# Transposing C for one of two weight tables with TensorE instead of the DMA queue, in a four-layer SSM kernel

## The chip, the cores and the metric

The kernel runs on one core of a Trainium2 chip. The metric is the device time of one execution in microseconds. Each core has TensorE (PE, matrix multiply), VectorE (DVE), ScalarE (ACT), GpSimd (POOL) and SyncE (SP, which here only issues DMA), with two on-chip memories: SBUF, and PSUM, into which PE writes its results.

## The reference, cut to what matters

Four layers alternate over a sequence of 2048 tokens with 640 features, in bfloat16: A, B, A, B. Each begins with a layer norm and adds its result to its input.

```python
def _A_ref(x, Lambda_re, Lambda_im, B_re, B_im, C_re, C_im, log_dt, Dskip):
    Lam_bar = jnp.exp(dt * Lam)                               # one complex number for each state
    B_bar = ((Lam_bar - 1.0) / Lam)[:, None] * Bmat
    Bu = jnp.einsum("bld,pd->blp", x + 0j, B_bar)
    for t in range(L):
        h = Lam_bar[None, :] * h + Bu[:, t, :]
        hs.append(h)
    return 2.0 * jnp.einsum("blp,dp->bld", hseq, Cmat).real + x * Dskip

def _B_ref(q, k, v, shift_k, ssm_k, ssm_D):
    kv = (short convolution of k with shift_k) * v
    y = (long convolution of kv with ssm_k, by FFT) + kv * ssm_D
    return q * y

x = x + _A_ref(_layernorm(x), ...)      # A1
x = x + _B_ref(_layernorm(x), ...)      # B1
x = x + _A_ref(_layernorm(x), ...)      # A2
x = x + _B_ref(_layernorm(x), ...)      # B2
```

Both A layers have the same parameters, and both B layers the same k, v and filters, so the long convolution y is computed once.

## The kernel before

The kernel has three stages, which overlap. The set-up makes tables of the parameters of A. The y passes (five, of 128 features each) compute the long convolution with matrix products. Then the layers run, each in four chunks of 512 tokens.

In layer A the recurrence runs over pairs of tokens. It needs the transposed B in two forms (BT0, BT1), two tables of C, transposed and scaled (W0 and W1), a product of W0 with B (G0), and tables of cosines and sines (tab, rtab). All are made once and used by every chunk. W0 and W1 each have a real and an imaginary part, of five blocks of 128 rows; each block is a column block of C, transposed, in a linear combination of its real and imaginary parts with one scalar per row. In the kernel before, each block of C is transposed by the DMA on its way in, separately for W0 and W1:

```python
    R_wr = Ring(St["b5"], 2, lambda t: (t[:, 0:2 * D].rearrange("p (c d) -> p c d", c=2), t[:, 2 * D:4 * D].bitcast(F32)))
    def weights(w, after):
        made = []
        for j in range(NJ):
            s_wr = R_wr.new()
            t_wl = []
            for c, src in ((0, A_C_re), (1, A_C_im)):
                def e_wl(_, c=c, src=src, j=j, s_wr=s_wr):
                    nc.sync.dma_start_transpose(out=s_wr.get()[0][:, c, :], in_=src[:, j * P:(j + 1) * P])        # L549
                t_wl.append(S.add(f"a_wl{w}{j}:{c}", "sp", 1.2, t_go, e_wl, xt=0.8, uses=[s_wr]))
            for c in range(2):
                def e_wc(...):
                    nc.scalar.activation(s_wr.get()[1], s_wr.get()[0][:, 1, :], ACT.Copy, scale=st["F6"][:, w, c + 1, j:j + 1])   # L553
                ...
                def e_wm(...):
                    nc.vector.scalar_tensor_tensor(aw["W1" if w else "W0"][:, c, j, :], s_wr.get()[0][:, 0, :],
                                                   st["F6"][:, w, c, j:j + 1], s_wr.get()[1], ALU.mult, ALU.add)          # L557
                ...
    w0s = weights(0, [])
    ...                                   # B transposed (a_b0, a_b1), then G0 from W0 and B (a_gm, a_ge)
    w1s = weights(1, gms)
```

B is loaded in whole rows and transposed by TensorE: a matmul with B as the stationary operand and the identity as the moving one (L573). Before the layers need them, W1[:, 0] and tab serve as homes of B, which is needed until the a_gm products are made; W1 is written after those.

PSUM is four buffers of 128 x 1024 f32. A matmul group takes one, and the copy out of it to SBUF, by ACT (L383) or DVE (L385), gives it back:

```python
def evac(nc, eng, out, in_):
    if eng == "act":
        nc.scalar.activation(out, in_, ACT.Copy)        # L383
    else:
        nc.vector.tensor_copy(out, in_)                 # L385
```

Other lines that are named below: L1172 is the short convolution of k and L1178 its product with v; L1217, L1241 to L1246, L1322/1323 and L1351 are matmuls of the y passes; L771 and L774 are the input products of layer A, L809 its scan and L860 its output products; L868 and L872 take the output products out of PSUM, L872 with the residual.

Each engine works through its own instructions in order. This order is made when the program is built. Every operation has a name and a number in a table; a list scheduler with estimated durations takes the operation that is ready and has the lowest number. Where an operation may run on two engines, a second number says how long to wait for the first:

```python
WHEN = {
    "warm": -3.83, "yt_io0": 2.11, ..., "a_wl00:0": 32.6, "a_wl00:1": 49.01, ..., "B2c3_st:3": 348.96,
}
```

The end of the program is the last chunk of layer B2. It is done in four sub-chunks, each of which waits for one output group (A2c3_cp) of layer A. Sub-chunks 0 to 2 normalise (L727 on ACT), multiply by y (L924 on DVE) and add x (L932 on DVE or GpSimd, for the last two chunks). Sub-chunk 3 has two fused DVE instructions (L909, L913), of which only the second needs the reciprocal (L692). Each sub-chunk is stored by its own DMA.

Of the kernel before, what the change touches and what calls it, by code (L numbers as in the profile page):

```python
# [9 lines left out]
ALU = mybir.AluOpType  # L10
# [7 lines left out]
P = 128  # L18
# [34 lines left out]
    "warm": -3.83, "yt_io0": 2.11, "yt_ph0": 2.86, "yt_sin0": 5.82, "yt_neg0": 16.74, "yt_io6": 1.83, "yt_ph6": 8.35, "yt_sin6": 13.55, "yt_neg6": 16.04,  # L53
    "yt_io12": 8.66, "yt_ph12": 10.58, "yt_sin12": 11.04, "yt_neg12": 16.39, "yt_Ci": 8.52, "yt_Si": 23.89, "yt_nsi": 31.06, "yt_f0": 1.21, "yt_f2": 6.25,
    "yt_f3": 9.49, "yt_f4": 8.15, "yt_h0": 0, "yt_h1": -0.99, "yt_h2": 5.01, "yt_h3": 5.6, "kv_dsl": 2.5, "kv_kd": 0.96, "kv_k0": 5.85, "kv_k1": 6.47,
    "kv_k2": 9.75, "kv_d0": 9.95, "kv_d1": 10.69, "kv_d2": 9.55, "kv_ds0": 12.7, "kv_lk0": -2.5, "kv_lv0": 12.92, "kv_mm0:0": 14.98, "kv_ev0:0": 17.09,
    "kv_mm0:1": 16.97, "kv_ev0:1": 19.32, "kv_st0": 19.31, "kv_ds1": 14, "kv_lk1": 18.02, "kv_lv1": 17.66, "kv_mm1:0": 20.91, "kv_ev1:0": 23.08,
    "kv_mm1:1": 22.64, "kv_ev1:1": 25.83, "kv_st1": 34.93, "kv_ds2": 15.3, "kv_lk2": 38.27, "kv_lv2": 32.7, "kv_mm2:0": 46.93, "kv_ev2:0": 49.89,
    "kv_mm2:1": 47.83, "kv_ev2:1": 50.31, "kv_st2": 52.4, "kv_ds3": 29.13, "kv_lk3": 49.12, "kv_lv3": 44.01, "kv_mm3:0": 57.23, "kv_ev3:0": 59.86,
    "kv_mm3:1": 55.5, "kv_ev3:1": 57.95, "kv_st3": 89.09, "kv_ds4": 59.54, "kv_lk4": 63.8, "kv_lv4": 68.5, "kv_mm4:0": 72.02, "kv_ev4:0": 76.44,  # L60
    "kv_mm4:1": 69.17, "kv_ev4:1": 73.75, "kv_st4": 85.43, "a_pl": 0, "a_p0": 11.98, "a_p1": 12.7, "a_p2": 14.74, "a_p3": 15.74, "a_p4": 18.22, "a_p5":
    20.49, "a_p6": 24.21, "a_lamd": 24.71, "a_f": 26.96, "a_dd": 13.22, "a_ldB0": 7.86, "a_ldB1": -0.25, "a_wl00:0": 32.6, "a_wl00:1": 49.01, "a_wc00:0":
    52.65, "a_wm00:0": 55.99, "a_wc00:1": 58, "a_wm00:1": 59.08, "a_wl01:0": 36.12, "a_wl01:1": 41.24, "a_wc01:0": 46.96, "a_wm01:0": 39.62, "a_wc01:1":
    45.93, "a_wm01:1": 52.05, "a_wl02:0": 55.3, "a_wl02:1": 54.1, "a_wc02:0": 59.45, "a_wm02:0": 60.99, "a_wc02:1": 62, "a_wm02:1": 63.6, "a_wl03:0":
    61.4, "a_wl03:1": 62.6, "a_wc03:0": 66.32, "a_wm03:0": 72.97, "a_wc03:1": 74.16, "a_wm03:1": 75.66, "a_wl04:0": 66.1, "a_wl04:1": 67.3, "a_wc04:0":
    73.44, "a_wm04:0": 74.88, "a_wc04:1": 76.91, "a_wm04:1": 78.89, "a_b00:0": 24.39, "a_b0e0:0": (25.02, -1), "a_b00:1": 18.7, "a_b0e0:1": (19.33, 99),
    "a_b00:2": 19.83, "a_b0e0:2": (19.91, 3), "a_b00:3": 24.96, "a_b0e0:3": (25.65, 99), "a_b00:4": 41.45, "a_b0e0:4": (42.57, 1.5), "a_b01:0": 7.78,
    "a_b0e1:0": (8.33, 99), "a_b01:1": 11.2, "a_b0e1:1": (17.24, 3), "a_b01:2": 8.91, "a_b0e1:2": (10.1, 1.5), "a_b01:3": 7.5, "a_b0e1:3": (8.91, 6),
    "a_b01:4": 9.82, "a_b0e1:4": (10.46, 99), "a_b10:0": 31.05, "a_b1e0:0": (32.11, 3), "a_b10:1": 34.44, "a_b1e0:1": (35.71, 1.5), "a_b10:2": 34.09,
    "a_b1e0:2": (34.05, 6), "a_b10:3": 29.71, "a_b1e0:3": 30.83, "a_b10:4": 26.83, "a_b1e0:4": (28.08, 99), "a_b11:0": 29.02, "a_b1e1:0": (29.24, 3),  # L70
    "a_b11:1": 38.81, "a_b1e1:1": (39.48, 6), "a_b11:2": 27.39, "a_b1e1:2": (28.66, 0), "a_b11:3": 32.04, "a_b1e1:3": (33.19, 3), "a_b11:4": 41.73,
    "a_b1e1:4": (43.23, 1.5), "a_gm0": 79.89, "a_ge0": (82.96, 0.8), "a_gm1": 89.66, "a_ge1": (93.72, 0.8), "a_gm2": 103.17, "a_ge2": (105.9, 99),
    "a_gm3": 93.91, "a_ge3": (98.25, 3), "a_gm4": 87.15, "a_ge4": (89.6, 3), "a_wl10:0": 78.7, "a_wl10:1": 102.7, "a_wc10:0": 110.77, "a_wm10:0": 114.1,
    "a_wc10:1": 125.39, "a_wm10:1": 133.68, "a_wl11:0": 87.7, "a_wl11:1": 84.7, "a_wc11:0": 89.2, "a_wm11:0": 106.96, "a_wc11:1": 113.29, "a_wm11:1":
    114.88, "a_wl12:0": 125.81, "a_wl12:1": 127, "a_wc12:0": 129.1, "a_wm12:0": 131.85, "a_wc12:1": 129.33, "a_wm12:1": 134.54, "a_wl13:0": 136.24,
    "a_wl13:1": 134.55, "a_wc13:0": 138.41, "a_wm13:0": 143.56, "a_wc13:1": 145.4, "a_wm13:1": 150.76, "a_wl14:0": 142.49, "a_wl14:1": 144.61, "a_wc14:0":
    148.81, "a_wm14:0": 150.98, "a_wc14:1": 153.51, "a_wm14:1": 155.99, "a_ti": 21.15, "a_ta": 22.89, "a_t0": 28.86, "a_t1": 116.09, "a_t2": 118.28,
    "yq0_kl": 4.7, "yq0_ka": 10.39, "yq0_KA:m0": 13.91, "yq0_KA:e0": (14.91, 0), "yq0_KA:m1": 16.88, "yq0_KA:e1": (17.73, 0.8), "yq0_KA:m2": 11.55,
    "yq0_KA:e2": (12.48, 0), "yq0_KA:m3": 11.83, "yq0_KA:e3": (13.61, 0.8), "yq0_KB:m0": 19.69, "yq0_KB:e0": (21.5, 0.8), "yq0_KB:m1": 25.93, "yq0_KB:e1":
    (27.18, 3), "yq0_KB:m2": 27.95, "yq0_KB:e2": (30.14, 99), "yq0_KB:m3": 19.26, "yq0_KB:e3": (20.51, -1), "yq0_KB:m4": 24.73, "yq0_KB:e4": (26.28, 99),  # L80
    "yq0_vl": 20.25, "yq0_VA:m0": 31.93, "yq0_VA:e0": (32.86, 0.8), "yq0_VA:m1": 31.61, "yq0_VA:e1": (31.78, -1), "yq0_VA:m2": 33.58, "yq0_VA:e2": (33.88,
    0.8), "yq0_VA:m3": 33.17, "yq0_VA:e3": (34.03, -1), "yq0_VB:m0": 36.93, "yq0_VB:e0": (37.23, 0), "yq0_VB:m1": 34.74, "yq0_VB:e1": 35.93, "yq0_VB:m2":
    34.86, "yq0_VB:e2": (38.43, 3), "yq0_VB:m3": 38.85, "yq0_VB:e3": (40.09, 3), "yq0_VB:m4": 40.15, "yq0_VB:e4": (40.99, 99), "yq1_kl": 28.9, "yq1_ka":
    35.09, "yq1_KA:m0": 39.77, "yq1_KA:e0": (40.4, -1), "yq1_KA:m1": 40.48, "yq1_KA:e1": (41.28, 0), "yq1_KA:m2": 34.56, "yq1_KA:e2": (36.44, 1.5),
    "yq1_KA:m3": 38.26, "yq1_KA:e3": 39.21, "yq1_KB:m0": 47.16, "yq1_KB:e0": (48.45, 0), "yq1_KB:m1": 43.41, "yq1_KB:e1": (45, 6), "yq1_KB:m2": 44.31,
    "yq1_KB:e2": (45.9, 6), "yq1_KB:m3": 42.51, "yq1_KB:e3": (40.68, 1.5), "yq1_KB:m4": 45.2, "yq1_KB:e4": (47.91, 0), "yq0_pw": 44.47, "yq0_IB:m0":
    41.73, "yq0_IB:e0": (50.06, 0), "yq0_IB:m1": 53.02, "yq0_IB:e1": (54.27, 0), "yq0_IB:m2": 50.53, "yq0_IB:e2": (53, 3), "yq0_IB:m3": 52.12,
    "yq0_IB:e3": (53.37, 6), "yq0_IB:m4": 51, "yq0_IB:e4": (52.12, 6), "yq0_tt": 56.5, "yq1_vl": 40.21, "yq1_VA:m0": 55.2, "yq1_VA:e0": (57.1, 3),
    "yq1_VA:m1": 52.74, "yq1_VA:e1": (53.85, -1), "yq1_VA:m2": 54.63, "yq1_VA:e2": (55.97, 0), "yq1_VA:m3": 54.92, "yq1_VA:e3": (56.77, 0), "yq1_VB:m0":
    61.7, "yq1_VB:e0": (62.72, 0.8), "yq1_VB:m1": 59.86, "yq1_VB:e1": (61.1, 99), "yq1_VB:m2": 60.8, "yq1_VB:e2": 62.14, "yq1_VB:m3": 58.96, "yq1_VB:e3":  # L90
    60.2, "yq1_VB:m4": 62.41, "yq1_VB:e4": (63.27, -1), "yq0_IA:m0": 65.86, "yq0_IA:e0": (70.73, 99), "yq0_IA:m1": 65.37, "yq0_IA:e1": 67.04, "yq0_st":
    73.4, "yq2_kl": 46.52, "yq2_ka": 53.61, "yq2_KA:m0": 63.88, "yq2_KA:e0": (64.52, 1.5), "yq2_KA:m1": 62.99, "yq2_KA:e1": (63.62, 99), "yq2_KA:m2":
    63.6, "yq2_KA:e2": (64.38, 0), "yq2_KA:m3": 64.76, "yq2_KA:e3": (65.42, 1.5), "yq2_KB:m0": 66.7, "yq2_KB:e0": (67.94, -1), "yq2_KB:m1": 71.13,
    "yq2_KB:e1": (72.54, 0), "yq2_KB:m2": 68.27, "yq2_KB:e2": (69.89, 6), "yq2_KB:m3": 67.37, "yq2_KB:e3": 68.99, "yq2_KB:m4": 69.96, "yq2_KB:e4": 72.04,
    "yq1_pw": 65.51, "yq1_IB:m0": 77.79, "yq1_IB:e0": (78.82, 99), "yq1_IB:m1": 76.23, "yq1_IB:e1": (77.63, 0.8), "yq1_IB:m2": 74.65, "yq1_IB:e2": (75.9,
    0), "yq1_IB:m3": 73.75, "yq1_IB:e3": (75, 3), "yq1_IB:m4": 75.82, "yq1_IB:e4": (78.53, 6), "yq1_tt": 79.9, "yq2_vl": 70.8, "yq2_VA:m0": 79.49,
    "yq2_VA:e0": (80.74, -1), "yq2_VA:m1": 78.92, "yq2_VA:e1": (80.07, 1.5), "yq2_VA:m2": 79.2, "yq2_VA:e2": (80.63, 99), "yq2_VA:m3": 77.13, "yq2_VA:e3":
# [313 lines left out]
def a_setup_tasks(S, nc, wp, St, consts, t_go, A_Lambda_re, A_Lambda_im, A_B_re, A_B_im, A_C_re, A_C_im, A_log_dt, A_Dskip, after_sin):  # L411
# [130 lines left out]
    def weights(w, after):  # L542
        made = []
        for j in range(NJ):
# [6 lines left out]
            for c in range(2):  # L551
                def e_wc(_, w=w, c=c, j=j, s_wr=s_wr):
                    nc.scalar.activation(s_wr.get()[1], s_wr.get()[0][:, 1, :], ACT.Copy, scale=st["F6"][:, w, c + 1, j:j + 1])  # L553
# [998 lines left out]
```

## Time and profile before

| | us |
|---|---|
| median of three executions | 363.18 |
| lowest, highest | 362.35, 363.43 |
| span of the profiled execution | 361.4 |
| PE busy | 334.2 |
| DVE busy | 315.6 |
| ACT busy | 257.2 |
| transposes of C (DMA): 20 | median 3.9 (real part), 2.9 (imaginary) from issue to landing |
| whole loads of B (800 KB each): 2 | 7.5 and 8.9 from issue to landing |

The page cuts the span into 40 equal slices and writes the busy share of each engine in a slice as a digit of tenths. PE is busy in nearly all slices; the DMA row has nines in the first third and low digits in the second half. A row of the wait list names an engine and line that waited, what ended the wait, the total in microseconds, how often, and the longest. A row of a timeline gives the start, the duration, the engine, the line and the operation.

### The profile page before, as it was taken

How to read it: one execution, taken by the hardware profiler on the slowest of the kernel's cores; microseconds unless marked ns; L12 is line 12 of the kernel's file. 1: busy time of each engine (PE TensorE's matmuls, PEld its weight loads, DVE VectorE, ACT ScalarE, POOL GpSimd, SP SyncE). 2: the span in 40 equal slices, each digit the busy share in tenths (PEclk: the TensorE clock that was granted, in tenths of full speed). 3: DMA queues.
4: the chain of work that ended last, by engine and by line, in shares of the span. 5: the costliest groups of instructions: out<-in, count | busy, mean ns of one | idle time of the engine just before them, and what ended most of it. 6: DMA issues, size and time to landing. Idle time of an engine off the chain costs nothing.

```text
span 361.4 us, 8447 instructions
## 1 busy us (share of the span) xinstructions
PE 334.2 (92%) x3565; PEld 250.6 (69%) x3565; DVE 315.6 (87%) x477; ACT 257.2 (71%) x408; POOL 25.7 (7%) x54
## 2 busy tenths in 40 slices
PE   7599699988999898998999999999999999999980
PEld 7457687666777798996686686697856866856640
DVE  8889589898298889999998969797989959999896
ACT  3979597898699999882259676994198395404872
POOL 5634002000000000000000000000000000000041
PEclk9789699999999999999999999999999999999996
DMA  7999988999999991696206690515006004130042
GB/s 193 215 193 191 204 153 170 170 150 224 203 300 199 213 170 31 119 190 143 73 3 96 148 353 18 127 30 136 2 2 145 3 0 74 38 109 3 25 169 98
DMA packets 119000, 45.91 MB, mean 127 GB/s; under 512 B 111661, under 2 KB 113458, under 8 KB 118962
## 3 DMA queue, kind: packets, MB, share of 16 engines
q1 hardware_dynamic: 118816, 45.36, 58.4%
q8 instruction: 28, 0.46, 0.5%
q14 instruction: 10, 0.08, 0.1%
q10 hardware_dynamic: 146, 0.01, 0.0%
HBM read 17.38 MB, written 7.86 MB: 70 GB/s over the span
## 4 chain that ended last, share of the span: by engine, by line
PE 57%; ACT 5%; DMA 2%; DVE 1%; issue 1%; ACTq 0%
PE ps L860 33%; PE ps L771 10%; PE ps L774 10%; ACT b L383 2%; DMA b<-b 2%; PE ps L1322 1%; PE ps L1323 1%; DVE b L932 1%; ACT rtab L649 0%; ACT tab L647 0%; PE ps L1241 0%; ACT L645 0%; ACT tab L645 0%; PE ps L1217 0%; ACT rtab L646 0%
## 5 line engine op out<-in xcount | busy, mean ns | idle before, releaser
L383 ACT ACTIVATE b<-ps 128x1024 bf16<-128x1024 f32 (+2 forms) x123 | 106.0, 923 | 36.6 <-PE ps L774 26.2
L860 PEld LDWEIGHTS <-b 128*128 128x128 bf16 x880 | 67.9, 98 | 48.3
L860 PE MATMUL ps<-W,b 128*128 128x128 bf16 (+1 forms) x640 | 96.1, 299 | 0.0
L771 PE MATMUL ps<-b,BT 128*128 128x256 bf16 x400 | 56.8, 273 | 1.2 <-DMA b<-b 1.0
L774 PE MATMUL ps<-b,BT 128*128 128x256 bf16 x400 | 56.7, 273 | 0.0
L809 DVE TENSOR_TENSOR_SCAN b<-rtab,b 128x1290 bf16<-128x1290 f32 x16 | 44.7, 2832 | 0.2
L771 PEld LDWEIGHTS <-BT 128*128 128x128 bf16 x400 | 38.4, 98 | 5.8 <-DMA b<-b 1.3
L774 PEld LDWEIGHTS <-BT 128*128 128x128 bf16 x400 | 39.2, 98 | 4.5
L727 ACT ACTIVATE b<-b,nmr,rstd 128x640 bf16<-128x640 f32 (+1 forms) x44 | 37.5, 911 | 6.4 <-DVE nmr L694 6.4
L682 ACT ACTIVATE junk<-b,nmean 128x640 bf16<-128x640 f32 x48 | 39.7, 828 | 1.5
L1241 PE MATMUL ps<-b,b 128*128 128x128 bf16 x170 | 35.6, 222 | 3.2 <-ACT b L383 2.7
L385 DVE CAST b<-ps 128x1024 bf16<-128x1024 f32 (+1 forms) x26 | 30.3, 1188 | 8.2 <-PE ps L1246 5.2
L1244 PE MATMUL ps<-b,b 128*128 128x128 bf16 x170 | 35.9, 222 | 0.0
L1243 PE MATMUL ps<-b,b 128*128 128x128 bf16 x150 | 33.4, 223 | 0.0
L1246 PE MATMUL ps<-b,b 128*128 128x128 bf16 x150 | 33.4, 222 | 0.0
L860 PE MATMUL ps<-G,b 128*128 128x512 bf16 (+1 forms) x160 | 27.0, 299 | 0.0
L932 POOL TENSOR_TENSOR b<-b,b 128x640 bf16<-128x640 bf16 x3 | 5.6, 1877 | 283.9 <-DVE b L924 283.9
L868 ACT ACTIVATE b<-ps 128x640 f32<-128x640 f32 x15 | 10.5, 699 | 21.5 <-PE ps L860 21.4
L1172 PE MATMUL ps<-b,fd 128*128 128x512 bf16 x80 | 20.3, 405 | 1.1 <-DVE b L385 0.8
L1322 PE MATMUL ps<-b,b 128*128 128x128 bf16 x160 | 19.2, 219 | 1.7 <-DVE b L1178 1.6
L1217 PE MATMUL ps<-FA,b 64*128 64x128 bf16 x320 | 15.3, 228 | 5.1 <-DVE b L385 2.8
L1323 PE MATMUL ps<-b,b 128*128 128x128 bf16 x160 | 19.1, 219 | 0.0
(212 smaller groups left out, 582.3 us busy)
## 6 DMA issues: line engine op xcount, KB each, us to landing
b<-in_A_x_dram SPq DMA_DIRECT2D x8, 640.0 KB, 4.4
b<-ysd SPq DMA_DIRECT2D x8, 640.0 KB, 5.3
b<-in_B_ssm_k_dram SPq DMA_DIRECT2D x5, 512.0 KB, 7.0
kvd<-b SPq DMA_DIRECT2D x5, 512.0 KB, 3.9
b<-kvd SPq DMA_DIRECT2D x5, 512.0 KB
ysd<-b SPq DMA_DIRECT2D x5, 512.0 KB, 3.9
out_dram<-b SPq DMA_DIRECT2D x6, 320.0 KB, 2.2
W<-in_A_B_im_dram SPq DMA_DIRECT2D x1, 800.0 KB, 7.5
```

What stands on the lines that cost most here:

```text
L383: nc.scalar.activation(out, in_, ACT.Copy)
L385: nc.vector.tensor_copy(out, in_)
L682: nc.scalar.activation(small.junk, src(q), ACT.Square, bias=st["nmean"][:, i:i + 1], scale=1.0, accum_out=st["ssq"][:, i:i + 1])
L727: nc.scalar.activation(dst, src, ACT.Identity, bias=st["nmr"][:, i:i + 1], scale=st["rstd"][:, i:i + 1])
L771: nc.tensor.matmul(pb[:, jj, c2, :], lhsT=aw["BT1"][:, c2, j, k, :], rhs=uT[:, 0:2, k, :], start=(k == 0), stop=False)
L774: nc.tensor.matmul(pb[:, jj, c2, :], lhsT=aw["BT0"][:, c2, k, j * P:(j + 1) * P], rhs=uT[:, 2:4, k, :], start=False, stop=(k == NJ - 1))
L809: nc.vector.tensor_tensor_scan(gv, rt, gv, 0.0, ALU.mult, ALU.add)
L860: nc.tensor.matmul(pc[:, o0:o1], lhsT=lh, rhs=rh, start=(n == 0), stop=(n == len(ops) - 1))
L1241: nc.tensor.matmul(ps[:, g, 0, :], lhsT=T["Cf"].get()[:, q, :], rhs=are, start=True, stop=single)
L1243: nc.tensor.matmul(ps[:, g, 0, :], lhsT=T["Sf"].get()[:, q, :], rhs=A[:, 2 * q + 1, :], start=False, stop=True)
L1244: nc.tensor.matmul(ps[:, g, 1, :], lhsT=T["NSf"].get()[:, q, :], rhs=are, start=True, stop=single)
L1246: nc.tensor.matmul(ps[:, g, 1, :], lhsT=T["Cf"].get()[:, q, :], rhs=A[:, 2 * q + 1, :], start=False, stop=True)
```

## The change

The ten transposing loads for W0 go. C's two parts are loaded once in whole rows, into the places where G0 and W1[:, 1] will be written later. For each of five blocks TensorE transposes both parts with the identity, five 128 x 128 pieces each, into two PSUM buffers. ACT scales the imaginary part straight out of one, and DVE combines it with the real part straight out of the other. W1 keeps its own ten transposing loads. The aim is to relieve the DMA queue and the SP queue during the set-up and the y passes.

```diff
+    C = (aw["G0"], aw["W1"][:, 1])
+    t_cl = []
+    for i, src in ((0, A_C_re), (1, A_C_im)):
+        def e_cl(_, src=src, i=i):
+            nc.sync.dma_start(out=C[i][:], in_=src.rearrange("(k p) e -> p k e", p=P))
+        t_cl.append(S.add(f"a_ldC{i}", "sp", 0.5, [], e_cl, xt=2.2))
+
+    R_w0 = Ring(St["b5"], 1, lambda t: t[:, 0:4 * D].bitcast(F32).rearrange("p (c d) -> p c d", c=2))
+    w0s = []
+    for j in range(NJ):
+        s_t, pcs = R_w0.new(), [R_ps.new(), R_ps.new()]
+
+        def e_ct(_, j=j, pcs=pcs):
+            for c in (1, 0):
+                for k in range(NJ):
+                    nc.tensor.matmul(pcs[c].get()[:, k * P:(k + 1) * P], lhsT=C[c][:, k, j * P:(j + 1) * P], rhs=ident[:], start=True, stop=True)
+        t_ct = S.add(f"a_ct{j}", "pe", c_mm(P, 10), t_cl, e_ct, uses=[s_t] + pcs)
+        for c in range(2):
+            def e_wc(_, c=c, j=j, s_t=s_t, s_pc=pcs[1]):
+                nc.scalar.activation(s_t.get()[:, c], s_pc.get()[:, 0:D], ACT.Copy, scale=st["F6"][:, 0, c + 1, j:j + 1])
+            t_wc = S.add(f"a_wc0{j}:{c}", "act", c_act(D), [t_ct, t_f], e_wc, uses=[s_t, pcs[1]])
+
+            def e_wm(_, c=c, j=j, s_t=s_t, s_pc=pcs[0]):
+                nc.vector.scalar_tensor_tensor(aw["W0"][:, c, j, :], s_pc.get()[:, 0:D], st["F6"][:, 0, c, j:j + 1], s_t.get()[:, c], ALU.mult, ALU.add)
+            w0s.append(S.add(f"a_wm0{j}:{c}", "dve", 0.77, [t_wc], e_wm, uses=[s_t, pcs[0]]))
...
-    def weights(w, after):
+    def weights1(after):
...                                        (its body, for W1 only)
-    w0s = weights(0, [])
...
-    w1s = weights(1, gms)
+    w1s = weights1(gms)
```

The table of numbers is new in every entry, so the order on every engine is new, from the start to the end of the program, and 65 operations of two possible engines change sides. The table's part of the diff is left out here. What it does to the order, as far as the prediction speaks of it:

```
SP, before     kv_lk0 a_ldB1 yq0_kl a_ldB0 kv_lv0 kv_lv1 kv_lk1 ... yq1_kl a_wl00:0 kv_lv2 kv_st1 a_wl01:0 kv_lk2 yq1_vl a_wl01:1 kv_lv3 ...
SP, after      a_ldB1 a_ldB0 yq0_kl kv_lk0 kv_lk1 kv_lv0 kv_lv1 ... yq1_kl kv_st1 kv_lv2 a_wl10:0 kv_lk2 yq1_vl a_wl10:1 kv_lk3 a_ldC1 a_wl11:1 kv_lv3 a_ldC0 ...
PE, after      ... yq1_KA:m1 a_b11:4 kv_mm2:0 yq1_KB (5 groups) kv_mm2:1 ... kv_mm3:1 a_ct0 yq1_VB (5 groups) a_ct1 yq2_KA ... kv_mm4:0 a_ct2 kv_mm4:1 ... yq2_VA a_ct3 yq2_VB:m1 m2 m3 a_ct4 ...
PE, end        before  A2c2_cp:3 A2c3_cp:3 A2c3_cp:1 A2c3_cp:2 A2c3_cp:0
               after   A2c2_cp:3 A2c3_cp:1 A2c3_cp:0 A2c3_cp:2 A2c3_cp:3
GpSimd, end    before  B2c2_m:3 B2c2_m:0 B2c31_m:1
               after   B2c2_m:3 B2c2_m:0 B2c30_m:0 B2c31_m:1
DVE, end       before  ... A2c3_xe:0 B2c31_mm B2c32_mm B2c32_m:2 B2c33_u:3 B2c30_ln_post B2c33_m:3 B2c30_mm B2c30_m:0
               after   ... A2c3_xe:3 B2c30_mm B2c31_mm B2c32_mm B2c32_m:2 B2c33_u:3 B2c33_ln_post B2c33_m:3
```

## The prediction

> **What bounds the kernel now.** I read the page's busy line first, then the busy slices, then a table of the span by stretches, then the waits of TensorE, then the end of the chain.
>
> ```profile
> span 361.4 us, 8447 instructions
> PE 334.2 (92%) x3565; PEld 250.6 (69%) x3565; DVE 315.6 (87%) x477; ACT 257.2 (71%) x408; POOL 25.7 (7%) x54
> PE   7599699988999898998999999999999999999980
> DMA  7999988999999991696206690515006004130042
> 20.00:120.00 100.00, 91.13 (x1256) 70.53 (x1255) 80.72 (x133) 83.88 (x114) 8.15 (x16) 0.96 1.01 196
> 120.00:170.00 50.00, 47.41 (x617) 41.96 (x617) 48.09 (x62) 42.30 (x54) 0.00 (x0) 1.00 0.74 147
> 170.00:351.40 181.40, 181.40 (x1561) 126.86 (x1558) 163.53 (x220) 114.02 (x218) 4.01 (x2) 1.00 0.30 77
> 351.40:361.40 10.00, 0.00 (x0) 0.00 (x0) 6.69 (x11) 3.14 (x6) 1.59 (x1) 0.71 0.27 98
> ```
>
> The last four rows give, for a stretch, the busy time of PE, PEld, DVE, ACT, POOL, then the granted clock, the DMA share and GB/s. From 170 to 351.4 us PE is busy for all 181.4 us: nothing can shorten that stretch except fewer matmul columns. Everything else lies outside it: 10.0 us of tail with no matmul, 8.9 us of PE idle in 20 to 120, 2.6 us in 120 to 170, and 5.8 us in the first 20 (the same table for that stretch shows 14.2 us of PE busy). In 20 to 120 the DMA share is 1.01: the queue is full there, and the diff takes work out of just that stretch. Who holds PE up there?
>
> ```profile
> PE ps L1217 <- DVE b L385: 2.8, 1, 2.8
> PE ps L1241 <- ACT b L383: 2.7, 7, 0.5
> PE ps L1322 <- DVE b L1178: 1.6, 3, 1.1
> PE ps L771 <- DMA b<-b: 1.0, 1, 1.0
> ```
>
> Three of the four wait for an engine that empties PSUM (L383 and L385 are the copy helper), one for a transfer. So a full DMA queue is seldom PE's direct releaser; it acts through what arrives late and bunches the evacuations.
>
> The first of these waits, at 36.4 to 39.2 us, costs more than its 2.8 us. After it the 128-column matmuls start 107 ns apart until 45.0 us, before and later 55.6 ns: about 49 matmuls at 51 ns more, 2.5 us.
>
> **What the skill says.** "TensorE: Matmul & The Clock Gate", Part 1, has matmuls of 128 columns 106.7 ns apart on a cold array and 55.6 ns on a warm one; the trace has both (107 and 55.6 ns). "Advanced Engine Details and Errata", X-Bar Transpose (TRN2), says that transpose DMAs are as fast as regular ones. This trace disagrees. In 132 to 141 us three transposes of C (each 640 x 128 bf16, 164 KB) are almost alone on the queue, and in 208.6 to 218.2 us four plain loads of 640 KB are:
>
> ```profile
> q1 hardware_dynamic: 3993, 0.99, 62.7%
> b<-in_A_C_im_dram SPq DMA_TRANSPOSE x2, 2.8
> b<-in_A_C_re_dram SPq DMA_TRANSPOSE x1
> ...
> q1 hardware_dynamic: 1304, 3.14, 89.2%
> b<-ysd SPq DMA_DIRECT2D x4, 640.0 KB, 7.1
> ```
>
> The first is 0.627 x 9 / 3 = at most 1.9 us of the whole queue for 164 KB (a little of an earlier load is in it); the second 0.892 x 9.6 = 8.6 us for 2.62 MB, 0.31 MB per us. Per byte the transpose costs 3.5 times as much. "SBUF — State Buffer", Who interferes with whom, says that a DVE instruction with two SBUF inputs and a GpSimd one that reads SBUF block each other. The trace agrees: the addition on L932 takes DVE 0.82 us alone and 1.91 us at 353.11, while GpSimd runs its own from 352.75.
>
> **The change part by part.**
>
> 1. Ten DMA transposes go (both parts of C, five column blocks, for W0 only; W1 keeps its ten). On the queue that is 10 x 1.9 = 19 us; two whole loads of C, 2 x 0.82 MB at 0.31, bring 5.3 us back. Relief 13.7 us in the 100 us where the queue is full. The SP queue sheds as much: the ten instructions take it 3.1 + 1.6 + 2.4 + 3.0 + 1.8 + 1.2 + 1.2 + 1.9 + 1.3 + 1.3 = 18.8 us between 31 and 77 us, against about 1.5 us for two loads like that of B_im (0.74 us). In the new program order four of W1's transposes move forward into the gap, so 8 to 9 us of queue time are really free before 80 us. Off PE's path; it lets kv and ssm_k inputs come earlier.
> 2. Fifty matmuls of 128 columns are added, 50 x 55.6 ns = 2.8 us. All before 90 us, but PE is the bound of the sum: unless they fall into present gaps they are on the path. Charge +2.8 us.
> 3. The scaling reads PSUM. ACT: ten of 0.852 us (L553) become ten like the f32 evacuation of 640 columns on L868 (0.699 us), -1.5 us. DVE: ten of 0.884 us (L557) become ten like L872, which also takes PSUM with an f32 tensor (0.818 us), -0.7 us. These two engines release PE's buffers in 60 to 160 us; where both are the limit, half of the 2.2 us, 1.1 us, could reach the end.
> 4. PSUM. Each block takes two of the four buffers at once and holds them for transposes, two ACT passes and a DVE pass behind each: 0.56 + 0.70 + 0.82 + 0.82, near 3 us with the handovers. Five times, the y passes have two buffers instead of four, and a 1024-column evacuation takes ACT 1.03 us. I charge 0.3 us each, +1.5 us in all.
> 5. The order of all engines is new; from 170 us on only a change of the PE work would matter, and there is none. Before that, PE loses 8.9 + 2.6 + 2.5 = 14.0 us. The new order has kv_mm2 and its evacuations in another place, so the wait of 2.8 us with its 2.5 us of slow clock has a good chance to go or shrink; other waits should shift more than vanish. I take 4 us of the 14.0 as recovered.
> 6. The start: B is loaded ahead of the first k transpose. PE waits 1.0 us for B_im there now. I take -0.3 us.
> 7. The tail. The last matmul now belongs to sub-chunk 3, whose sum is the fused pair on DVE, not to 0; and two additions instead of one go to GpSimd in this last chunk. Before:
>
> ```profile
> 352.54 0.83 ACT L682 ACTIVATE junk<-b,nmean 128x640 bf16<-128x640 f32 x1
> 353.11 1.91 DVE L932 TENSOR_TENSOR b<-b,b 128x640 bf16<-128x640 bf16 x1
> 354.94 0.87 DVE L909 SCALAR_TENSOR_TENSOR b<-b,nmean,b 128x640 bf16<-128x640 f32 x1
> 355.74 0.15 DVE L692 RECIPROCAL rstd<-std 128x1 f32<-128x1 f32 x1
> ```
>
> ACT has its statistics at 353.8, but DVE takes the reciprocal only at 355.7, then 356.1 to 358.4 goes to normalise (ACT 0.92), multiply (0.49) and add (0.82), and the store ends 3.0 us later. In the new order DVE has, from 352.3: three multiplies of 0.49, one addition of 0.82 to 1.91, the fused 0.87, reciprocal and product 0.3, the second fused 0.88: 4.3 to 5.4 us, to 356.6 to 357.7. That is 0.7 to 1.8 us less than 358.4; GpSimd will block some of it, so -1.0 us.
>
> Sum: +2.8 - 1.1 + 1.5 - 4.0 - 0.3 - 1.0 = -2.1 us; 363.2 - 2.1 = 361.1. The order was made for the new work, and the queue relief of part 1 has been given nothing by itself; a further 0.6 us for it gives 360.5 us.
>
> **The rivals.** (a) The queue relief counts in full: y passes start earlier, and most of the 14.0 us closes. Then 10 us are recovered in place of 4, and the time is near 354. For it: share 1.01 over 100 us. Against it: three of four PE waits name an evacuation, and DVE and ACT are busy 48.1 and 42.3 of the 50 us after 120. (b) The transposes stall PE, which works in order: block 0 stands behind kv_mm3 and needs both loads of C, issued late between k and v transposes; loads of 0.8 MB took 7.5 and 8.9 us to land in the crowded start. A wait over some 3 us would also bring the slow clock of 39 us back. Then +3 to +5 us: 364 to 366. For it: that very thing happens at 39 us now. Against it: the load's issue precedes kv_lv3's use and other PE work. (c) PSUM is starved as in part 4 but more, 1 us or more per block: 364.
>
> **Range and chances.** The floor: closing all 14.0 us and 1.0 of the tail, with 2.8 of matmuls added, gives 363.2 - 14.0 - 1.0 + 2.8 = 351. The plausible range is set by (a) at 354 and by (b) and (c) at 364 to 366; 356.0 to 365.0 should hold it 8 times in 10. Faster by over 2% is under 355.9 and needs (a) nearly whole: 0.10. Slower by over 2% is over 370.4 and needs (b) and (c) together: 0.03. Within 2%: 0.87.
>
> **What would show it.** PE busy over 170 us to its end unchanged in rate, with no gaps; fifty more matmuls on PE starting 55.6 ns apart; ten fewer transposes of C and a DMA share under 1.0 in 40 to 80 us; PE idle plus slow clock in 20 to 170 us of about 10 us in place of 14.0; the wait at 36 us gone or short; tail near 9.0 us. The prediction is wrong if PE waits several us for the loads of C at the first transposes, if waits on evacuations grow around the five blocks, or if the gaps before 170 us close to under 6 us.

## The result and the profile after

| | before | after |
|---|---|---|
| median, us | 363.04 | 359.08 |
| lowest to highest, us | 362.35 to 363.43 | 358.43 to 360.18 |
| span of the profiled execution, us | 361.4 | 357.1 |
| last matmul ends at, us | 351.4 | 346.4 |
| from there to the end, us | 10.0 | 10.7 |

The ratio of the times is 0.9896, with a 95% interval of 0.9866 to 0.9926: 4.0 us less where 2.7 were predicted. The two lower rows already tell that errors cancelled in the sum: the last matmul is 5.0 us earlier, the tail (the time behind it) 0.7 us longer. They come from one execution of each kernel; in a second execution of the changed one (x_again below) the last matmul ended at 347.2 us and the tail was again 10.7.

The page of the kernel after, busy line and slices:

```profile
span 357.1 us, 8548 instructions
...
PE 333.7 (93%) x3615; PEld 250.6 (70%) x3615; DVE 308.6 (86%) x471; ACT 263.8 (74%) x413; POOL 24.1 (7%) x55
...
PE   7698899799999999999999999999999999999970
...
DMA  8989999999958909952664722507023030120152
```

PE has its fifty more matmuls (3615 against 3565) and yet is not busy for longer. The DMA row still has its nines in the first third: much of what was taken out of the queue is filled with work that came forward.

The table by stretches of the kernel after (start:end, length, busy time of PE, PEld, DVE, ACT, POOL, granted clock, DMA share, GB/s):

```profile
20.00:120.00 100.00, 93.08 (x1351) 72.77 (x1351) 82.80 (x138) 91.98 (x121) 6.84 (x21) 0.99 0.94 199
120.00:170.00 50.00, 49.47 (x602) 41.04 (x600) 45.78 (x67) 44.75 (x58) 0.00 (x0) 1.00 0.61 122
170.00:346.40 176.40, 176.37 (x1533) 125.42 (x1529) 158.53 (x206) 109.65 (x210) 3.42 (x2) 1.00 0.32 81
346.40:357.10 10.70, 0.00 (x0) 0.00 (x0) 7.35 (x13) 3.27 (x8) 3.13 (x2) 0.63 0.32 123
40.00:90.00 50.00, 46.94 (x728) 38.33 (x726) 38.85 (x40) 45.56 (x55) 1.58 (x5) 1.00 1.08 216
```

The stretch from 40 to 90 us of the kernel before, for the last of these rows:

```profile
40.00:90.00 50.00, 45.88 (x642) 36.52 (x640) 41.22 (x41) 42.73 (x54) 2.25 (x6) 0.95 0.98 169
```

PE idle is 6.9 us in 20 to 120 (8.9 before) and 0.5 us in 120 to 170 (2.6 before), and the clock of 0.95 in 40 to 90 is 1.00. The losses of 14.0 us have become 7.4. From 170 us to the last matmul PE has no gap, as before; that stretch is 5.0 us shorter because more is done when it begins. From 20 to 120 us the DMA share fell from 1.01 to 0.94. In 40 to 90 us, where the loads were taken out, it has risen, and 216 GB/s arrive instead of 169: a queue as full as before delivers 28% more bytes, which fits the prediction's reading that a transposing load takes more queue time per byte.

How much is done when can be counted. Each matmul is taken at the spacing it has on a warm array (55.6 ns for 128 columns, 216 ns for 512, half for those of 64 rows), and the sum is taken by stretches:

| PE work started in, us | 0 to 60 | 60 to 120 | 120 to 170 | sum |
|---|---|---|---|---|
| before | 38.6 | 50.8 | 45.7 | 135.1 |
| after | 41.9 | 52.3 | 48.5 | 142.7 |

By 170 us the changed kernel has done 7.6 us more, of which 2.8 us are its own added transposes: 4.8 us ahead, which is the 5.0 us of the last matmul. Of the 7.6 us, 3.3 are gained before 60 us, where the kernel before had its wait of 2.8 us and its 2.5 us of slow clock, and where no transpose has run yet. The rows of PE's waits up to 175 us in the kernel after (line that waited, what ended the wait, total us, times, longest):

```profile
PE ps L1244 <- DVE b L385: 1.5, 2, 0.9
PE ps L1378 <- DMA b<-b: 1.1, 1, 1.1
PE ps L615 <- DVE b L488: 1.1, 1, 1.1
...
PE ps L1268 <- DVE b L385: 0.8, 2, 0.5
...
PE ps L557 <- ACT b L383: 0.5, 1, 0.5
```

L1244, L1268 and L1378 are L1217, L1241 and L1351 of before. The wait of 2.8 us is gone; the largest single one here is 1.1 us. It went because PE has other groups in front of it now: DVE does the same steps of the tables from 35.0 to 37.9 us as before. L557 holds the new transposes: they wait for 0.5 us in all, for ACT at the fourth block, and not for their loads. C's two parts were issued at 46.4 and 53.3 us. The first landed after 6.4 us (of the second no landing is recorded), and the first transpose started at 62.4 us, with no wait in front of it.

The tail. The timeline of the kernel after (start, duration, engine, line, operation, in brackets the idle time before):

```profile
347.08 0.82 DVE L899 SCALAR_TENSOR_TENSOR b<-ps,b 128x640 f32<-128x640 f32 x1
...
347.82 2.50 DVE L951 TENSOR_TENSOR b<-b,b 128x640 bf16<-128x640 bf16 x3
...
348.44 3.13 POOL L959 TENSOR_TENSOR b<-b,b 128x640 bf16<-128x640 bf16 x2 [2.66 <-issue]
...
350.36 1.91 DVE L959 TENSOR_TENSOR b<-b,b 128x640 bf16<-128x640 bf16 x1
352.19 0.87 DVE L936 SCALAR_TENSOR_TENSOR b<-b,nmean,b 128x640 bf16<-128x640 f32 x1
...
353.24 0.88 DVE L940 SCALAR_TENSOR_TENSOR b<-b,rstd,b 128x640 bf16<-128x640 bf16 x1
```

L899, L951, L959, L936 and L940 are L872, L924, L932, L909 and L913 of before. GpSimd runs its two additions from 348.4 to 351.6, and in that time DVE takes 2.50 us for three multiplies of 0.49 and 1.91 us for an addition of 0.82: 2.1 us lost to save DVE two additions, 1.6 us. From the end of its last PSUM copy DVE works for 6.3 us, to 354.1; in the kernel before it was 6.2 us, from 352.2 to 358.4. The copy starts 0.7 us after the last matmul, where before it started at once (351.43 us), and that is the 0.7 us of the tail.

### The profile page after: what moved, and what is told of

Same layout as the page of the kernel before. It is cut to its first block, busy times and chain, and to the rows that moved or that the text cites. A ratio compares the mean times of both kernels' runs of the same rounds, so it can differ in the third digit from the quotient of the medians.

```text
span 357.1 us, 8548 instructions
## 1 busy us (share of the span) xinstructions
PE 333.7 (93%) x3615; PEld 250.6 (70%) x3615; DVE 308.6 (86%) x471; ACT 263.8 (74%) x413; POOL 24.1 (7%) x55
## 5 line engine op out<-in xcount | busy, mean ns | idle before, releaser
L383 ACT ACTIVATE b<-ps 128x1024 bf16<-128x1024 f32 (+3 forms) x127 | 113.2, 959 | 24.2 <-PE ps L801 19.7
L887 PEld LDWEIGHTS <-b 128*128 128x128 bf16 x880 | 67.7, 98 | 48.2
L754 ACT ACTIVATE b<-b,nmr,rstd 128x640 bf16<-128x640 f32 (+1 forms) x47 | 39.9, 909 | 6.1 <-DVE nmr L721 6.0
L1268 PE MATMUL ps<-b,b 128*128 128x128 bf16 x170 | 35.1, 219 | 1.3 <-DVE b L385 0.8
L1271 PE MATMUL ps<-b,b 128*128 128x128 bf16 x170 | 35.3, 219 | 0.0
L1273 PE MATMUL ps<-b,b 128*128 128x128 bf16 x150 | 32.8, 219 | 0.0
L1270 PE MATMUL ps<-b,b 128*128 128x128 bf16 x150 | 32.8, 219 | 0.0
L385 DVE CAST b<-ps 128x1024 bf16<-128x1024 f32 (+1 forms) x22 | 20.8, 966 | 8.1 <-PE ps L1273 3.7
L959 POOL TENSOR_TENSOR b<-b,b 128x640 bf16<-128x640 bf16 x4 | 6.6, 1660 | 281.7 <-DVE rstd L719 279.1
L1199 PE MATMUL ps<-b,fd 128*128 128x512 bf16 x80 | 21.0, 411 | 0.0
L1349 PE MATMUL ps<-b,b 128*128 128x128 bf16 x160 | 19.0, 219 | 0.5 <-ACT b L383 0.5
L1350 PE MATMUL ps<-b,b 128*128 128x128 bf16 x160 | 18.9, 219 | 0.0
L1268 PEld LDWEIGHTS <-b 128*128 128x128 bf16 x170 | 16.6, 98 | 1.3 <-DVE b L385 0.4
```

The lines of the kernel that those rows point to most:

```text
L754: nc.scalar.activation(dst, src, ACT.Identity, bias=st["nmr"][:, i:i + 1], scale=st["rstd"][:, i:i + 1])
L887: nc.tensor.matmul(pc[:, o0:o1], lhsT=lh, rhs=rh, start=(n == 0), stop=(n == len(ops) - 1))
L1199: nc.tensor.matmul(pk[:, 512 * b:512 * (b + 1)], lhsT=s_ds.get()[:, l, :], rhs=kT[:, t0:t0 + 512], start=(l == 0), stop=(l == 3))
L1268: nc.tensor.matmul(ps[:, g, 0, :], lhsT=T["Cf"].get()[:, q, :], rhs=are, start=True, stop=single)
L1270: nc.tensor.matmul(ps[:, g, 0, :], lhsT=T["Sf"].get()[:, q, :], rhs=A[:, 2 * q + 1, :], start=False, stop=True)
L1271: nc.tensor.matmul(ps[:, g, 1, :], lhsT=T["NSf"].get()[:, q, :], rhs=are, start=True, stop=single)
```

## The experiments

Four readings stood against each other. The order theory is the prediction's: the gain is the new order, above all the wait at 36 us that it avoids. The queue theory is rival (a): what counts is the relief of the DMA queue. The work theory says that the added matmuls, buffers and scalings cost what was charged, and the gain is so much larger elsewhere. The tail theory says that GpSimd's share in the last chunk gives what it was charged with.

| run | median, us | ratio to before | 95% interval |
|---|---|---|---|
| x_plain | 361.10 | 0.9965 | 0.9946 to 0.9985 |
| x_late | 361.69 | 0.9989 | 0.9963 to 1.0015 |
| x_late_plain | 360.37 | 0.9945 | 0.9926 to 0.9964 |
| x_path_only | 375.24 | 1.0363 | 1.0313 to 1.0414 |
| x_again (the changed kernel) | 359.00 | 0.9902 | 0.9876 to 0.9928 |
| x_back | 367.00 | 1.0125 | 1.0095 to 1.0154 |
| x_free | 359.20 | 0.9898 | 0.9872 to 0.9924 |
| x_twice | 360.20 | 0.9928 | 0.9903 to 0.9953 |
| x_w1_plain | 359.10 | 0.9903 | 0.9871 to 0.9935 |
| x_tail_dve | 358.79 | 0.9896 | 0.9865 to 0.9927 |
| x_tail_early | 358.31 | 0.9881 | 0.9846 to 0.9915 |
| x_tail_best | 358.44 | 0.9898 | 0.9866 to 0.9930 |

The median of the kernel before beside them was 362.3 to 362.8 us.

Where an edit says `move(name, before)`, it takes one operation out of the finished order and puts it ahead of another; nothing else moves.

### x_plain: the kernel before, with W0's loads of C plain

```diff
-                    nc.sync.dma_start_transpose(out=s_wr.get()[0][:, c, :], in_=src[:, j * P:(j + 1) * P])
+                    if w == 0:
+                        nc.sync.dma_start(out=s_wr.get()[0][:, c, :], in_=src[j * P:(j + 1) * P, :])
+                    else:
+                        nc.sync.dma_start_transpose(out=s_wr.get()[0][:, c, :], in_=src[:, j * P:(j + 1) * P])
```

The same bytes come in and all else stays; W0 is made from blocks that are not transposed, so this kernel leaves the transposition out. It gives the relief of the queue in the old order.

> The kernel before, in its own order, with the ten transposing loads of C for W0 replaced by ten plain loads of 128 rows of C each (the same bytes; W0 is then made of blocks that are not transposed, so the output is not the reference's). It takes about 13 us of queue work out of 30 to 80 us and adds no matmul. Queue theory: the relief is the gain of the change, so 2.5 to 5 us faster than before, 358 to 360.5. Order theory: TensorE waits for PSUM evacuations there and not for transfers, so within 1 us of before, 362 to 364.

Measured: 0.9965, so 1.3 us. The relief alone is worth something, but only a third of the change. The clock row was a surprise. The stretch after the wait at 36 us, first before, then x_plain:

```profile
39.30:45.00 5.70, 5.70 (x60) 5.11 (x60) 1.59 (x3) 3.35 (x4) 0.00 (x0) 0.50 0.94 134
```

```profile
39.30:45.00 5.70, 5.70 (x106) 5.18 (x106) 3.52 (x4) 5.02 (x6) 0.00 (x0) 1.00 0.87 170
```

Both executions have the same wait of 2.8 us just before. After it one runs at half clock and starts 60 matmuls in 5.7 us, the other at full clock and starts 106. The profile is one execution of each, and nothing in the kernels differs at that place but the kind of load. So part of the 3.3 us between these two spans is the clock. The 1.3 us is not: over all executions the mean granted clock was 0.974 in x_plain (22) and 0.976 in the kernel before (51), so x_plain is faster at a clock no higher.

### x_late: the kernel before, with the wait at 36 us taken out of the order

```diff
+        move("a_t0", "yq0_pw")
+        move("yt_nsi", "a_t0")
```

`a_t0` (a step of A's tables) and `yt_nsi` (a negated table) stand on DVE ahead of the copy that PE waits for at 36 us. They move behind it.

> The kernel before with two VectorE tasks moved later in VectorE's order and nothing else: the phase rounding for the cosine table (L639, L640) and the negated sine table (L1000), which stand ahead of two PSUM copies at 35 us, go behind the copies of the next groups. Order theory: the TensorE wait of 2.8 us at 36.4 us and the 5 us at half clock after it go, so the last matmul comes 3 to 5 us earlier: 358 to 360. Queue theory: TensorE only meets the next late transfer, so under 1 us: 362 to 363.5.

Measured: 0.9989, with 1 in the interval: the 3 to 5 us that the order theory put on this wait are not there. The profile is of the slowest of its fourteen executions (363.14 us). The wait at 36 us went, and another came. The timeline of PE and a stretch of x_late:

```profile
55.74 0.27 PE L1330 MATMUL ps<-b,b 128*128 128x128 bf16 x1 [2.87 <-DVE b L1310]
```

```profile
56.00:58.00 2.00, 2.00 (x22) 2.00 (x20) 2.00 (x3) 1.34 (x2) 0.94 (x2) 0.50 0.29 65
```

PE waits 2.87 us for the last step of the pointwise product of y pass 0 on DVE (L1310 here), and runs at half clock after it. DVE's own first and last step of that product:

```profile
47.74 1.28 DVE L1305 TENSOR_TENSOR b<-b,b 128x2176 bf16<-128x2176 bf16 x1
...
54.32 1.37 DVE L1310 TENSOR_TENSOR b<-b,b 128x2176 bf16<-128x2176 bf16 x1
```

In the kernel before the product started at 49.75 us: DVE is 2.0 us earlier in x_late, but PE is earlier by more, and DVE works without a pause from 43.7 us on. The two moved operations, 3.0 us of DVE's time, now stand straight in front of the product. What PE had gained at 36 it lost at 53, because the same engine owed it the next result too, not because a transfer was late. So moving DVE's work behind the wait is no gain by itself. The kernel after loses the wait in another way, by other PE work at that place, with DVE's order there as before; this run does not test that.

### x_late_plain: both together

> Both edits together: plain loads of C for W0 and the two VectorE tasks moved later. If the wait at 36 us and the queue each hold something of their own, the gains add: 5 us or more, 358 or less. If the order theory is all of it, the same as the later VectorE tasks alone, within 1 us.

The edits are those of the two runs above. Measured: 0.9945, 2.0 us. The interval overlaps that of x_plain, so a further gain from the moved wait is not shown. Relief and two moved operations together stay short of the change.

### x_path_only: the changed way to W0, in the old order

```diff
-    "a_wl00:0": 32.6, "a_wl00:1": 49.01, ... "a_wl04:1": 67.3,
+    "a_ldC1": 34.0, "a_ldC0": 35.0, "a_ct0": 44.9, "a_ct1": 51.6, "a_ct2": 58.4, "a_ct3": 65.3, "a_ct4": 72.4,
```

The code is that of the change, the table of numbers that of before, with entries for the new operations near where the old ones stood; the numbers of the first two blocks' scalings change places, as block 0 now comes first. Nothing is left out.

> The changed kernel's way of making W0 (two whole loads, TensorE transposes, scaling out of PSUM) with the numbers of the kernel before for every operation that both have; the new ones stand where the old loads and scalings stood. The list scheduler still moves some neighbours. Order theory: without the new order the added matmuls and the PSUM buffers show, so 0 to 4 us slower than before, 363 to 367. Queue theory: most of the gain is there already, 359 to 361.

Measured: 1.0363, 12.6 us slower. The waits up to 200 us in x_path_only (its L256 and L258 are the copies L383 and L385, L674 is L774, L1146 is L1246):

```profile
ACT b L256 <- PE ps L674: 16.6, 6, 3.8
...
DVE b L258 <- PE ps L1146: 9.4, 7, 4.1
```

The corresponding row of the kernel before is 6.2 us for ACT. The engines that empty PSUM now wait for PE, and PE is busy for 89.8 of the 100 us from 20 to 120 at a clock of 0.94. New operations in a list scheduler move many neighbours, so this run does not say which of buffers, loads or scalings does it. A part is the clock: its six executions had a mean of 0.960, the kernel before 0.976. It says that the code of the change needs an order made for it.

### x_again and x_back: the changed kernel, and with ten transposing loads put back

```diff
+        for j, pos in enumerate(("kv_lv2", "kv_lk2", "yq1_vl", "kv_lv3", "kv_lk3", "yq0_tt", "kv_lk4", "kv_lv4", "yq0_st", "yq2_vl")):
+            ...   # ahead of pos on SP: dma_start_transpose(out=spare[j % 2], in_=src[:, (j // 2) * P:(j // 2 + 1) * P])
```

x_again is the changed kernel once more, run beside its variants. x_back adds ten transposing loads of C, into buffers that nobody reads, in the changed kernel's own order. It carries more than the kernel before did: its ten transposes and also the two whole loads.

> The changed kernel unchanged, so that its variants have a partner on the same chip: near 359, about 0.990 of before.

> The changed kernel, its own order, with ten extra transposing loads of C put back into the SP queue at about the places where the old kernel had them, into a buffer that nobody reads. This undoes the queue relief alone. Plain loads in the old kernel gained 1.3 us, so by the theory that the relief is a part of the gain 1 to 3 us slower than the changed kernel. By the theory that the new order is all of it, and hides the queue, within 0.7 us.

Measured: 0.9902 and 1.0125. Ten loads that nothing depends on cost 8.0 us, several times what was expected. The waits of PE up to 175 us in x_back (L1213, L1357 and L1207 are L1205, L1349 and L1199 of after):

```profile
PE ps L1357 <- DVE b L1213: 2.3, 1, 2.3
...
PE ps L1386 <- DMA b<-b: 1.8, 1, 1.8
PE ps L1207 <- DVE b L1213: 1.5, 1, 1.5
```

Read alone, two of the three blame DVE. DVE's own timeline in x_back says what L1213 waited for:

```profile
61.08 1.22 DVE L1213 TENSOR_TENSOR b<-ps,b 128x1024 bf16<-128x1024 f32 x1 [2.97 <-DMA b<-in_B_v_dram]
...
83.50 1.22 DVE L1213 TENSOR_TENSOR b<-ps,b 128x1024 bf16<-128x1024 f32 x1 [2.49 <-DMA b<-in_B_v_dram]
```

The same two products in the kernel after:

```profile
59.35 1.22 DVE L1205 TENSOR_TENSOR b<-ps,b 128x1024 bf16<-128x1024 f32 x1 [1.23 <-PE ps L1199]
...
78.65 1.22 DVE L1205 TENSOR_TENSOR b<-ps,b 128x1024 bf16<-128x1024 f32 x1
```

The product of the short convolution with v holds a PSUM buffer until v has landed. In x_back it starts 1.7 us later, and the next one 4.9 us later. So the queue acts on PE through DVE: a transfer is late, DVE waits with a full buffer, and PE's row names DVE. These two waits are 3.8 of the 8.0 us; the rest was not followed to single waits.

"The queue" is two things here, SP, which issues the loads one after another, and the 16 DMA engines behind it. The issues of v for these two products, first x_back, then the kernel after:

```profile
53.89 3.54 SPq L1196 DMA_TRANSPOSE b<-in_B_v_dram  x1
...
78.61 2.09 SPq L1196 DMA_TRANSPOSE b<-in_B_v_dram  x1
```

```profile
48.40 4.80 SPq L1188 DMA_TRANSPOSE b<-in_B_v_dram  x1
...
72.80 3.36 SPq L1188 DMA_TRANSPOSE b<-in_B_v_dram  x1
```

The loads are 5.5 and 5.8 us late already when SP issues them. The ten added loads hold SP for 15.2 us, and from 40 to 90 us it is issuing for 47.6 of the 50 us. In x_again that is 38.7 us, while the DMA share is much the same, 1.13 against 1.10 in x_again, and so are the bytes, 215 against 214 GB/s. So the lateness is there before the transfer begins. Whether SP's own time for an issue is the limit, or full DMA engines that slow its issues, no run separates: x_plain relieves both, too (SP 31.9 us in place of 40.9, DMA share 0.90 in place of 0.98).

The kernel before had the first sign of it, in the waits of its DVE from 40 to 120 us:

```profile
DVE b L1178 <- DMA b<-in_B_v_dram: 1.3, 1, 1.3
```

L1178 is the very line that ended 1.6 us of PE's waits in the prediction's second view. The product that waited ran at 83.20 us, the next one at 85.93; 0.3 and 1.1 of the 1.6 us follow straight behind these two. In x_back PE has 88.6 us of work in 20 to 120 where x_again has 93.1.

### x_free and x_twice: the added work left out, and doubled

```diff
# x_free
+        order[:] = [t for t in order if not t.name.startswith(("a_ct", "a_wc0", "a_wm0"))]
-    C = (aw["G0"], aw["W1"][:, 1])
+    C = (aw["W0"][:, 0], aw["W0"][:, 1])
# x_twice
-            for c in (1, 0):
+            for c in (1, 0, 1, 0):
```

x_free loads C straight into W0 and leaves out the transposes, both PSUM buffers of each block and all ten scalings on each of ACT and DVE; the rest of the order stays. W0 then holds C as it is. x_twice does every transpose twice into the same buffers.

> The changed kernel with C loaded straight into W0 and the fifty transposes, ten ACT scalings and ten DVE combinations left out (the output is not the reference's); all other instructions in the same order. If the transposes and their PSUM buffers are on TensorE's path, as charged in the prediction (2.8 + 1.5 us, less the ACT and DVE work), 3 to 5 us faster than the changed kernel. If they fall into gaps, under 1.5 us faster.

> The changed kernel with each of the fifty transposes done twice into the same place: 2.8 us more TensorE work before 90 us and nothing else. On the path: 2 to 3 us slower than the changed kernel. In gaps: under 1 us.

Measured: 359.20 and 360.20 against 359.00. The whole of the new way to W0 costs nothing, within a margin of about 0.7 us estimated from the spread. The stretch from 60 to 120 us, in which it lies, first x_again, then x_free:

```profile
60.00:120.00 60.00, 55.94 (x813) 44.48 (x811) 49.86 (x75) 55.21 (x68) 0.11 (x1) 0.97 0.88 186
```

```profile
60.00:120.00 60.00, 53.95 (x772) 42.17 (x770) 42.50 (x65) 49.08 (x58) 0.11 (x1) 0.97 0.84 185
```

Without the work PE is busy for 2.0 us less, DVE for 7.4 and ACT for 6.1, and the kernel ends no sooner: all of it lay in time in which PE would have waited anyway, in x_free for copies by DVE and ACT (4.3 us) and for a transfer (1.8 us). Doubling adds 2.8 us of matmuls and 1.2 us of time. Six executions of each, side by side, took 359.70 to 360.60 us (x_twice) and 358.71 to 360.00 (x_again); their means are 1.0 us apart, with a margin of about 0.6 estimated from their spread. So the gaps hold the added work once, but not twice.

### x_w1_plain: W1's transposing loads plain as well

The edit is that of x_plain, for W1 in the changed kernel; W1 is then made from blocks that are not transposed.

> The changed kernel with the ten transposing loads of C that are left, those for W1, replaced by plain loads of as many bytes (the output is not the reference's). If the queue is still the limit between 40 and 90 us, 1 to 3 us faster than the changed kernel, 356 to 358. If the change has taken all that the queue had to give, within 0.7 us.

Measured: 0.9903, nothing. What C's loads for W0 took from the queue mattered; what those for W1 still take does not.

### x_tail_dve, x_tail_early and x_tail_best: the last chunk's additions

```diff
# x_tail_dve
+        for n in ("B2c30_m:0", "B2c31_m:1"):
+            next(t for t in order if t.name == n).eng = "dve"
+        move("B2c30_m:0", "B2c33_u:3")
+        move("B2c31_m:1", "B2c33_u:3")
# x_tail_early
+        next(t for t in order if t.name == "B2c30_m:0").eng = "dve"
+        move("B2c31_mm", "B2c2_m:2")
+        move("B2c31_m:1", "B2c2_m:2")
+        move("B2c30_m:0", "B2c32_m:2")
# x_tail_best: as x_tail_early, but
+        move("B2c31_mm", "B2c30_ln_post")
+        move("B2c31_m:1", "B2c30_ln_post")
```

The first takes GpSimd out of the last chunk. The other two leave it one addition, that of sub-chunk 1, and start it earlier, from a multiply that is moved ahead.

> The changed kernel with the two additions that GpSimd does in the last chunk (sub-chunks 0 and 1) given to VectorE, behind that of sub-chunk 2. VectorE gets 2 x 0.82 us of work more. If sharing with GpSimd is a saving, the tail of 10.0 us behind the last matmul grows by 1.6 us. If GpSimd only slows VectorE by as much as it takes off (the three multiplies took 2.50 us in place of 1.47, one addition 1.91 in place of 0.82), the tail stays within 0.5 us of 10.0, and the total is that of the changed kernel.

> The changed kernel with the multiply of sub-chunk 1 moved ahead of the last PSUM copy, so that GpSimd can do its addition before the tail, and the addition of sub-chunk 0 given to VectorE. VectorE then works alone behind the last matmul: 0.9 + 2 x 0.49 + 2 x 0.82 + 0.87 + 0.31 + 0.88, 5.6 us in place of 7.0. If the block between the two engines is what the prediction missed, the tail is 8.6 to 9.2 us and the total about 1 us below the changed kernel; if not, 10 us as before.

> As the run before with the early multiply, but the multiply of sub-chunk 1 goes ahead of the reciprocal and product of sub-chunk 0, so that GpSimd starts its addition about 0.8 us earlier and no longer holds up the product of sub-chunk 2 (1.17 us in that run, 0.16 us alone), which stood ahead of the last PSUM copy. If that block is what is left, the last copy starts about 0.9 us earlier and the total is 0.5 to 1 us under the run before, 357.3 to 357.8. If the last copy waits for the statistics of sub-chunk 2 on ScalarE anyway, no gain.

Measured: tails of 9.9, 9.7 and 10.1 us against 10.7. The timeline of x_tail_dve (L960, L968 and L945 are L951, L959 and L936 of after):

```profile
348.66 1.29 DVE L960 TENSOR_TENSOR b<-b,b 128x640 bf16<-128x640 bf16 x3
...
349.98 2.30 DVE L968 TENSOR_TENSOR b<-b,b 128x640 bf16<-128x640 bf16 x3
...
352.19 0.88 DVE L945 SCALAR_TENSOR_TENSOR b<-b,nmean,b 128x640 bf16<-128x640 f32 x1
```

All six instructions on DVE take 3.5 us, from 348.66 to 352.19; in the kernel after, four of them on DVE and two beside it on GpSimd take 4.4 us, from 347.82 to 352.19. Sharing lengthens this part. In the whole time that does not show: 358.79 us against 359.08. In the two versions with an earlier addition the block only moved. A small product that stands ahead of the last copy out of PSUM, first that of sub-chunk 2 in x_tail_early, then that of sub-chunk 0 in x_tail_best:

```profile
347.31 1.17 DVE L730 TENSOR_TENSOR nmr<-nmean,rstd 128x1 f32<-128x1 f32 x1
```

```profile
346.60 1.39 DVE L730 TENSOR_TENSOR nmr<-nmean,rstd 128x1 f32<-128x1 f32 x1
```

It takes 0.16 us when GpSimd is idle. Here it stands behind a GpSimd addition, and the last copy (347.08 in the kernel after) starts at 348.40 and 348.91. The lowest median of all runs is that of x_tail_early, but its interval contains the changed kernel's ratio. The changed kernel was not run beside it; x_w1_plain was, and took 0.8 us more. A small gain is possible, but no version that surely beats the changed kernel was found.

## Why the prediction was right, and where its steps were not

The total was right, and its sum was a balance of errors: the part up to the last matmul was predicted 1.7 us shorter with the 0.6 us for the queue and was 5.0 us shorter; the tail was predicted 1.0 us shorter and was 0.7 us longer. That these two errors have opposite signs is luck. The first is nearly all in steps 2 to 4: without their +3.2 us the terms up to the last matmul, -4.0, -0.3 and -0.6, make -4.9.

1. The queue. The mechanism was named in the prediction ("it acts through what arrives late and bunches the evacuations"), but then the relief was put "off PE's path" with 0.6 us. It is worth 1.3 us in the old order (x_plain), and putting a larger load back in the new one costs 8.0 us (x_back). Nor do the freed "8 to 9 us" come out of the step's own figures: 13.7 us less four transposes at 1.9 are 6.1 us. The reading failed because it followed PE's waits for one step: three rows that name an evacuation spoke against rival (a), and the one on L1178 was itself held by a transfer.
2. Steps 2 to 4, together +3.2 us (2.8 - 1.1 + 1.5), are the terms that failed outright: x_free measures 0 for all of them together. The prediction charged the matmuls "unless they fall into present gaps"; they do. Nor did the scaling get cheaper. ACT's took a median of 0.838 us (0.849 before, 0.70 assumed), DVE's 0.876 us (0.877 before, 0.82 assumed): other instructions of the same width that read PSUM were no model for these; why was not tried.
3. Step 5, -4.0 us for the order through the wait at 36 us. That wait is gone and the losses fell from 14.0 to 7.4 us, where about 10 were predicted. Of the 6.6 us that closed, 2.8 were filled by the transposes themselves; 3.8 are left, near the 4.0 taken. How much of them is the order's and how much the queue's was not separated. x_late takes the same wait out by DVE's order and gains nothing, so the wait alone was not worth its 2.8 us and the slow clock. Relief in the old order gives 1.3 us, the new way to W0 in the old order costs 12.6, and both in an order made for them give 4.0: the parts do not add. How much a new order alone would give with the old loads was not tried.
4. Step 6, the start. The count of work by 20 us is 8.2 against 7.9 us, so the -0.3 is about what is seen.
5. Step 7, the tail, -1.0 us. The term was mis-sized by 1.7 us: +0.7 measured. DVE's span from its last copy was put at 4.3 to 5.4 us and took 6.3, as long as before (6.2): GpSimd's block was counted for the addition, but it also holds up the three multiplies (2.50 us where 1.47 were counted), so the two additions taken from DVE are worth less than the block they bring. Left out, too, is that the copy itself starts 0.7 us after the last matmul, behind sub-chunk 2's statistics.
6. The rivals. (a) has its direction from x_plain and x_back, but not its size: it would have closed 10 of the 14.0 us and 6.6 were closed, with the new order's part in them. (b) fell: the transposes did not wait for C. (c) fell: PE's wait at the transposes is 0.5 us in all, and x_free gains nothing from the freed buffers.
7. The sign that was named and failed: a DMA share under 1.0 from 40 to 80 us. It is 1.04 there, and was 0.93 before. Later work came forward into the room that was made; what changed is what the queue delivers.

## What to carry to other kernels

Follow each wait of the bound engine back two steps: an evacuation that it names may itself stand waiting for a transfer, and then the queue is the bound although its row in the list is short. Where the bound engine has gaps, added work is free until they are full (the whole added path cost 0, its matmuls a second time 1.0 us), while removing one wait only moves it, if the engine that caused it owes the next result as well; and a change of structure needs an order made for it, or it can cost three times what it would bring. Before giving GpSimd a share of a tail, count what it takes from DVE's two-input instructions beside it (here 2.1 us lost for 1.6 saved).

## What the runs showed of the hardware

- After the same PE gap of 2.8 us one execution ran at half clock for 5.7 us (60 matmuls) and another at full clock (106). "TensorE: Matmul & The Clock Gate", Part 1, puts the drop after an idle window of about 3.4 us and says that this window runs free, so that the number of slow matmuls at a kernel's start varies from run to run. The runs here show that the drop varies as well, and that it can follow a gap shorter than that figure. Half clock in one profile is then a weak ground for a prediction of 2.5 us.
- A GpSimd addition held up even a DVE product of one element per partition: 0.16 us became 1.17 and 1.39 us. That is the lock that "SBUF — State Buffer", Who interferes with whom, describes, and its price is the length of the GpSimd instruction that remains, not the size of the one that waits.
- Ten transposing loads of 164 KB that nothing reads cost 8.0 us of a 359 us kernel, though no engine ever waits for one of them. They held SP for 15.2 us, and the loads of v behind them were issued 5.5 and 5.8 us later.
